# Earlier loads of keys and queries, a new schedule of the row-maxima steps and later value weights in a two-layer transformer kernel

## The chip, the cores and the metric

The kernel runs on one core of one Trainium2 chip. The metric is device time in microseconds (us) from launch to end; lower is better. The profile shows one execution, engine by engine: PE (TensorE matmuls), PEld (TensorE weight loads), DVE (VectorE), ACT (ScalarE), POOL (GpSimd), and SP, whose queue issues nearly all DMAs here.

## What is computed

The reference runs two equal layers over `x` of shape 1 x 2048 x 640 in float32. A layer is an attention block with 32 heads of 20 and an MLP:

```python
def _A_ref(x, wqkv, wo):
    qkv = (x @ wqkv).reshape(B, S, 3, H, Dh)   # transposed to 3, B, H, S, Dh
    q, k, v = qkv[0], qkv[1], qkv[2]
    scores = einsum("bhqd,bhkd->bhqk", q, k) * Dh ** -0.5
    p = softmax(scores)
    return einsum("bhqk,bhkd->bhqd", p, v) ... @ wo

x = x + _A_ref(_layernorm(x), wqkv, wo)
x = x + _B_ref(_layernorm(x), w1, b1, w2, b2)      # relu(x @ w1 + b1)^2 @ w2 + b2
x = x + _A_ref(...); x = x + _B_ref(...)           # once more, with the same weights
```

## The kernel before

A layer has three stages: the projections (`qkv`), the attention proper (`attention`), and output projection with MLP. Each float32 operand of the projections is split into a high and a low part, and three products are summed. Intermediate queries, keys and values go to DRAM (`d_qk`, `d_kd`, `d_v`) and come back in the layouts that later stages need.

**Softmax maxima.** The kernel subtracts the true row maximum inside the exponential: the maximum is an added row of the query operand of the score matmul. So every score is computed twice, first with queries on the partitions to take maxima (`by_queries`, L561; reduced on DVE, L573), then with keys on the partitions for the exponentials (`score`, L657; ACT, L664). Heads are taken in 8 groups of four (g), queries in 4 blocks of 512 (qb), keys in 4 chunks of 512 (c); `t = 4 g + qb` numbers a block of the attention, and 16 key tiles `kt` make one block.

**Maxima during the projections.** A part of the maxima is computed already during the projections. A triple (g, qb, c) is a *group* of 8 steps, each of two matmuls (one for each row half of the array). With c a number it is *plain*: two matmuls, two DVE reductions (`smax_two`, L587). With "d" or "e" it is *double* and serves two key chunks (0 and 1, or 2 and 3): the matmuls of a first half-step multiply queries with key differences `kd` and ACT writes their relu (`step_two`, L595); the second half-step multiplies with the lower chunk's keys and DVE adds the relu and takes the maximum (`both_two`, L602). `DOUBLE` holds 22 double groups of the head groups 0, 1 and 2.

**What sets the order.** The instruction order is written out by program. `qkv` walks 40 units (tb, pos), a token block with one of ten 128-column pieces of queries and keys, 15 matmul products each (n = 0 to 39), and then 16 value units of 30 products. From unit 4 on a product is two half-height matmuls, the second 22 products behind the first (`halves` L358, `catch` L367). After every product `between(cost)` (cost 1, or 0.65 in value units) lowers a pace counter; when it is used up `some()` issues one maxima step and adds `PLAIN_PACE` or `DOUBLE_PACE`. `following` takes the next group off a list and calls `tiles`, which issues the loads of its keys and queries (`load_k`, `load_q`, `load_kd`: six DMAs of 80 KB each, on SP) and also those of the following group, or of the following two while not all token blocks are transposed. `end_group` gives tiles up that no later group needs. `LISTED` and `PLAIN` say after which unit groups are listed. What is stored (`d_qk`, `d_kd`, `d_v`) is put on SP 10 products after its unit ended (`later`). After the last projection `while begun` drops the double groups that were not begun.

**Queues and tiles.** SP takes its DMAs in the order in which the program recorded them and stops at the first whose semaphores are not yet there. Tiles of keys, queries, split weights and evicted projections share one pool of 42 slots of 8 KB a partition; a new tile waits for the last reader of the slot that it gets.

**The attention.** `attention` interleaves scores (`a`, `b`), value products (`V`, L669) and the maxima that are still to do (`m`, `n`; the list `todo`), by the strings in `ORDERS`. `begin(i)` issues loads: at every fourth key tile of a head group's first block the keys of head groups ahead (`load_k`), and the keys of group 3 in block 1.

Of the kernel before, what the change touches and what calls it, by code (L numbers as in the profile page):

```python
# [25 lines left out]
NQB = S // QB  # L26
# [13 lines left out]
def tile_layers(  # L40
# [26 lines left out]
    def slot(shape, dtype, label):  # L67
        return arena.tile(shape, dtype, tag="slot", name=name(label))
# [132 lines left out]
    w_v = Split("wv", HALF, KD * 4)  # L201
# [15 lines left out]
    def raw_rows(src, k):  # L217
        raw = xtile("raw")
        dma(nc.sync, raw, src[k * P : (k + 1) * P, :])
        return raw  # L220
# [121 lines left out]
    xt_, keys = {}, {}  # L342
# [162 lines left out]
    left, done, split = {}, set(), {}  # L505
# [12 lines left out]
    def load_k(g, c, keep):  # L518

        if not keep:  # L520
            k = slot([P, 2, QB], F32R, "k")
        elif (g % 4, c) in kept:
            k = kept[g % 4, c]
        else:
            k = kept[g % 4, c] = slot([P, 2, QB], F32R, "k")
            for par in range(2):
                dma(nc.sync, k[64 * par + 60 : 64 * par + 62], d_one)
        k_t[g, c] = k
        rows_of_heads(k, d_qk[1, :, :, c * QB : (c + 1) * QB], KSEG, g)

    def load_q(t):
        g, qb = divmod(t, NQB)
        q_t[t] = slot([P, 2, QB], F32R, "q")
        rows_of_heads(q_t[t], d_qk[0, :, :, qb * QB : (qb + 1) * QB], QSEG, g)
# [202 lines left out]
    def prep_job():  # L737
# [12 lines left out]

    PLAIN = [
        ([(0, 0, 0)], [(1, 0, 0)]),
        ([(0, 0, 1)], [(1, 0, 1)]),
        ([], []),
        ([], []),
    ]
    DOUBLE = [
        [],  # L760
# [9 lines left out]

    FIRST = 4
    PLAIN_PACE = 4.2
    DOUBLE_PACE = 2.1
    LISTED = {11: 1, 14: 2, 18: 3}
    UNITS = [(tb, pos) for tb in range(NQB) for pos in range(FIRST)]
    UNITS += [(tb, pos) for pos in range(FIRST, 10) for tb in range(NQB)]

    def qkv(first, x_src, rest):

        pending, groups, work = [], [], []  # L780
        double, twos, begun = [], [], []
        left.update((t, 4) for t in range(NBLK))
        done.clear()
        state = {"pace": 0, "n": 0}
        early, late, later_rows = {}, {}, []
        coming = [y for x in DOUBLE for y in x if y[2] == "d"]

        def at(when, n, f):
            when.setdefault(n, []).append(f)

        for pos in range(2 if first else FIRST, 10):
            n = UNITS.index((0, pos)) - 4 if pos >= FIRST else pos - 2
# [8 lines left out]
        for k in range(KD if first else w_v.n):  # L801
            n = len(UNITS) - 7 + k
            if first:
                at(early, n - 2, lambda k=k: raws.append(raw_rows(wqkv[:, 2 * D :], k)))
                at(late, n, lambda k=k: w_v.put(
                    raws.pop(0), k * 4, k * 4 + 2, 2, nc.scalar.copy, pool_lo
                ))
            else:
                at(early, n, lambda k=k: w_v.load(k))

        def begin(when, n):
            for f in when.pop(n, ()):
                f()

        def later(f):
            pending.append((state["n"] + 10, f))

        def settle(n):
            while pending and pending[0][0] <= n:
# [2 lines left out]
        def tiles(x):  # L822
            g, qb, c = x
            for c in [c] if c in range(4) else [c, 2 * "de".index(c)]:
                if (g, c) not in k_t:
                    if c in range(4):
                        load_k(g, c, g > 1)
                    else:
                        load_kd(g, c)
            if g * NQB + qb not in q_t:  # L830
                load_q(g * NQB + qb)

        def end_group(x):
            g, qb, c = x
            t = g * NQB + qb
            rest = groups + double + [w[0] for w in work + twos] + [w[0][0] for w in begun]
            if t == 0:
                left[t] -= 1 if c in range(4) else 2
                if left[t] == 0:
                    mrows_max(t)  # L840
                    mrows(t)
                    later_rows.append(t)
            if (t or left[t]) and all(y[:2] != (g, qb) for y in rest):
                del q_t[t]
            use = {(y[0], y[2]) for y in rest + coming}
            use |= {(h, 2 * "de".index(y)) for h, y in use if y not in range(4)}
            for y in [y for y in k_t if y[0] == g and y not in use]:
                if g < 2 or y[1] not in range(4):
                    del k_t[y]

        def following(todo, queue):

            if not queue:
                if not todo:
                    return None
                x = todo.pop(0)
                tiles(x)
                for y in todo[: 2 if len(xt_) < NQB else 1]:
                    tiles(y)
                queue.extend((x, p, sub) for p, sub in PAIRS)  # L860
            return queue.pop(0)
# [10 lines left out]
        def some():  # L872
# [4 lines left out]
            if begun and (len(begun) > 1 or not (double or twos)):  # L877
# [6 lines left out]
                if (p, sub) == PAIRS[-1]:  # L884
                    end_group(w[0])
                return DOUBLE_PACE
            if groups or work:
# [3 lines left out]
            if w:  # L891
                (g, qb, x), p, sub = w
                begun.append((w, step_two(g * NQB + qb, p, sub, x)))
            return DOUBLE_PACE

# [11 lines left out]
        for n, (tb, pos) in enumerate(UNITS):  # L907
            while tb not in xt_:
                next(rest)
            begin(early, n)  # L910

            def end(store, n=n, tb=tb, pos=pos):
                later(store)
                if pos >= FIRST and tb == NQB - 1 or n == 4 * FIRST - 1:
                    w_qk.past(pos * 10 + 9, w_qk.got)

            proj_unit(pos, tb, run, run.whole if n < FIRST else run.halves, end)
            begin(late, n)
            if 2 < n < NQB * FIRST + 3:
                b, step = divmod(n - 3, 4)  # L920
                have, new = groups, PLAIN[b][step // 2]
                if step % 2:
                    have.extend(new)
                elif new:
                    tiles(new[0])
                if step == 2 and DOUBLE[b]:
                    tiles(DOUBLE[b][0])
            if n in LISTED:
                double.extend(DOUBLE[LISTED[n]])
                coming[:] = [y for y in coming if y not in double]  # L930
            if first:
                w_qk.save_full(1)
                w_v.save_full(1)
        for tt in range(NKT):

            def end(store, tt=tt):
                later(store)
                if tt % 4 == 3:
                    del xt_[tt // 4]

            v_unit(tt, run, end)
            if first:
                w_v.save_full(1)
            if tt == 10:
                load_v(0, 0)
            if tt == 12:
                for c in range(4):
                    assert (0, c) not in k_t
                    load_k(0, c, True)
                load_q(1)  # L950
        while run.behind:
            run.catch()
        while begun:
            del double[:], twos[:]
            some()
        w_v.drop()
        w_qk.drop()
# [22 lines left out]
    def attention(first, x_src, first_rows):  # L980
# [5 lines left out]
        state = {"begun": -1, "done": 0, "acc": None, "debt": 0, "st": ps_st}  # L986
        sm_ring = Ring(4, 5, 6)
        todo = [
            (t, p, sub, c)
            for t in range(NBLK)  # L990
            for c in range(4)
            for p, sub in PAIRS
            if (t, p, sub, c) not in done
        ]
# [13 lines left out]
        def begin(i):  # L1008

            t, u = divmod(i, NKT)  # L1010
            g, qb = divmod(t, NQB)
            if u == 1:
                q_t.pop(t - 1, None)
                if t + 2 < NBLK and t + 2 not in q_t:
                    load_q(t + 2)
            if u % 4 == 1 and qb == 0:
                k_t.pop((g - 1, u // 4), None)
                for h in (0, 1, 2, 3) if g else (0, 1, 2):
                    if g + h < NG and (g + h, u // 4) not in k_t:
                        load_k(g + h, u // 4, True)  # L1020
                if g and g + 3 >= NG:
                    del kept[(g - 1) % 4, u // 4]
            if t == 1 and u % 4 == 1:
                load_k(3, u // 4, True)
            if u in (2, 10) and qb == NQB - 1 and g + 1 < NG:
                load_v(g + 1, u // 8)
            if first and t < 16 and u % 6 == 3:
                prep_job()
            if first and t < 16 and u == 8:
                for sp in (w_o, w_1, w_2):  # L1030
                    sp.save_full()
                    sp.past(sp.count, sp.got)
            if (t, u) in loads:
                loads[t, u]()
            if t == NBLK - 1 and u == 12:
                first_rows.extend(row_tile(x_src, i) for i in range(4))
            if i in split:
                split.pop(i)()
# [300 lines left out]
```

## Time and profile before

| | |
|---|---|
| time, median of 3 runs | 3780.71 us (3778.38 to 3782.02) |
| the profiled execution: time / span | 3779.25 us / 3777.3 us |
| span, first layer: projections / attention / rest | 0 to 380 / to 1490 / to 1905 us |
| span, second layer: projections / attention / rest | to 2262 / to 3362 / to 3777 us |
| PE busy in these six stretches | 338.30, 1075.71, 408.97, 328.12, 1072.84, 409.22 us |
| ACT busy in the two attentions | 1043.02, 1042.79 us |
| granted PE clock in the six stretches | 0.96, 0.98, 1.00, 0.95, 0.98, 1.00 |

Idle time of an engine that does not set the end costs nothing. A wait is put down to the instruction or DMA that ended it; "q<-d_qk" is the load of a query tile. "Granted clock" is the share of full speed that TensorE was given.

### The profile page before, as it was taken

The page shows a single profiled execution, that of the slowest core. Times are in us where ns is not written, and L with a number is a line of the kernel's source. Part 1 is how long each engine was busy: PE and PEld are TensorE (multiplying, and loading weights), DVE is VectorE, ACT ScalarE, POOL GpSimd, SP SyncE. Part 2 cuts the span into 40 slices and gives each one's busy share as a digit, 9 for nine tenths or more (in the row PEclk, how much of TensorE's full clock was granted, in tenths as well). Part 3 has the DMA queues.
Part 4 walks back from the last instruction along what each step waited for, and adds up shares of the span by engine and source line. Part 5 has one row for each costly group of instructions (what it writes and reads, how often), then busy time and mean ns, then how long its engine had stood idle before and what let it go on. Part 6 is the DMA issues. An engine that isn't in the chain of part 4 may idle for free. (4 is left out here: it accounts for less than half of the span.)

```text
span 3777.3 us, 69873 instructions
## 1 busy us (share of the span) xinstructions
PE 3633.2 (96%) x25492; PEld 2202.4 (58%) x25492; DVE 2667.9 (71%) x5208; ACT 2698.9 (71%) x5298; POOL 867.0 (23%) x993
## 2 busy tenths in 40 slices
PE   7989799999999999999989897999999999999999
PEld 5879234444444444988878792444444444359898
DVE  7869488888888882444468784888888888814443
ACT  2768699999999997122217686999999999951221
POOL 6530134321111221111254200211112122111220
PEclk9999899999999999999999898999999999999999
DMA  6654454432222135722246543222222221357221
GB/s 212 203 195 134 112 150 144 156 101 62 69 59 56 47 92 158 285 85 70 91 144 213 162 133 86 72 64 67 80 58 65 56 57 49 95 188 256 70 71 41
DMA packets 277992, 425.92 MB, mean 113 GB/s; under 512 B 70228, under 2 KB 129364, under 8 KB 277648
## 3 DMA queue, kind: packets, MB, share of 16 engines
q1 hardware_dynamic: 277104, 419.73, 35.7%
q8 instruction: 202, 3.31, 0.4%
q10 hardware_dynamic: 544, 1.71, 0.2%
q14 instruction: 142, 1.16, 0.1%
HBM read 276.62 MB, written 144.68 MB: 112 GB/s over the span
## 5 line engine op out<-in xcount | busy, mean ns | idle before, releaser
L664 ACT ACTIVATE e<-banks 128x512 f32<-128x512 f32 x4096 | 2085.8, 614 | 120.4 <-PE banks L657 80.5
L573 DVE TENSOR_REDUCE mx<-banks 128x1 f32<-128x512 f32 x2624 | 1657.7, 685 | 385.2 <-PE banks L561 348.3
L669 PE MATMUL banks<-e,vg 128*32 128x512 f32 x8192 | 1098.8, 609 | 11.9 <-ACT e L664 11.9
L657 PE MATMUL banks<-q,k 62*128 62x512 f32 x4096 | 1076.0, 446 | 2.3 <-DVE mx L602 2.0
L657 PEld LDWEIGHTS banks<-q,k 62*128 62x128 f32 x4096 | 574.4, 185 | 854.3 <-ACT e L664 772.3
L561 PE MATMUL banks<-k,q 60*128 60x512 f32 x3424 | 1000.2, 414 | 63.2 <-DMA k<-d_qk 47.2
L561 PEld LDWEIGHTS banks<-k,q 60*128 60x128 f32 x3424 | 496.7, 188 | 193.1 <-DVE mx L573 101.3
L602 DVE CUSTOM_DVE_ANT_0 rl<-banks,rl 128x512 f32<-128x512 f32 x672 | 436.7, 689 | 102.1 <-PE banks L561 64.6
L595 ACT ACTIVATE rl<-banks 128x512 f32<-128x512 f32 x672 | 366.2, 600 | 114.1 <-PE banks L561 89.5
L669 PEld LDWEIGHTS banks<-e,vg 128*32 128x32 f32 x8192 | 161.6, 108 | 337.4 <-issue 281.3
L338 PE MATMUL banks<-w,h 128*128 128x320 f32 x2304 | 349.3, 310 | 2.7 <-DVE h L259 2.5
L338 PEld LDWEIGHTS banks<-w,h 128*128 128x128 f32 x2304 | 339.3, 188 | 11.4 <-DVE h L259 6.4
L1187 ACT ACTIVATE r<-banks,b_t 128x512 f32<-128x512 f32 x96 | 66.2, 689 | 382.1 <-PE banks L338 232.6
L358 PE MATMUL banks<-xnT,wqk 64*128 64x512 f32 x1080 | 337.8, 407 | 0.0
L367 PE MATMUL banks<-xnT,wqk 64*128 64x512 f32 x1080 | 336.6, 404 | 0.1
L338 PE MATMUL banks<-xnT,w 128*128 128x512 f32 x1440 | 331.5, 391 | 0.0
L338 PEld LDWEIGHTS banks<-xnT,w 128*128 128x128 f32 x1440 | 270.7, 189 | 55.7
L561 PE MATMUL banks<-kd,q 60*128 60x512 f32 x672 | 211.0, 408 | 34.2 <-DMA q<-d_qk 15.4
L713 POOL TENSOR_TENSOR few<-few,minus_t 128x16 f32<-128x16 f32 x62 | 179.9, 2901 | 198.5 <-DMA few<-d_s 198.5
L270 POOL CAST mr<-nt 128x32 fp32r<-128x32 f32 x64 | 13.5, 211 | 915.6 <-DVE nt L628 915.6
L724 POOL TENSOR_TENSOR o<-o 128x512 f32<-128x512 f32 x62 | 79.6, 1284 | 612.1 <-DMA o<-d_r 347.9
L367 PEld LDWEIGHTS banks<-xnT,wqk 64*128 64x128 f32 x1080 | 208.1, 193 | 15.1 <-DVE turned_t L360 0.5
(88 smaller groups left out, 2923.8 us busy)
## 6 DMA issues: line engine op xcount, KB each, us to landing
q<-d_qk SPq DMA_DIRECT2D x792, 80.0 KB
d_qk<-ev SPq DMA_DIRECT2D x80, 512.0 KB
k<-d_qk SPq DMA_DIRECT2D x456, 80.0 KB
x<-d_x SPq DMA_DIRECT2D x96, 320.0 KB
d_o<-ot SPq DMA_DIRECT2D x248, 80.0 KB
ot<-d_o SPq DMA_DIRECT2D x38, 512.0 KB
d_v<-v SPq DMA_DIRECT2D x32, 512.0 KB
vg<-d_v SPq DMA_DIRECT2D x32, 512.0 KB
```

The lines of the kernel that those rows point to most:

```text
L338: nc.tensor.matmul(dst, a, b, start=(n == 0), stop=(n == last))
L358: nc.tensor.matmul(dst, a[:64], b[:64], start=start, stop=last)
L367: nc.tensor.matmul(dst, a, b, start=False, stop=last, skip_group_check=True)
L561: nc.tensor.matmul(dst, q_t[t][b : b + 60, p, sub * P : (sub + 1) * P], k_t[t // NQB, c][b : b + 60, p, :], start=True, stop=True,)
L573: nc.vector.tensor_reduce(maxima(t)[:, 2 * p + par, sub, c : c + 1], dst, axis=AX.X, op=ALU.max)
L595: nc.scalar.activation(r, dst, AF.Relu)
L602: nc.vector.tensor_tensor_reduce(out=r[par], in0=dst, in1=r[par], scale=1.0, scalar=LEAST, op0=ALU.add, op1=ALU.max, accum_out=maxima(t)[: ...
L657: nc.tensor.matmul(dst, k_t[t // NQB, kt // 4][b : b + 62, p, (kt % 4) * P : (kt % 4 + 1) * P], q_t[t][b : b + 62, p, :], start=True, stop ...
L664: nc.scalar.activation(es[p][:, par, :], dst, AF.Exp, scale=SCALE)
L669: nc.tensor.matmul(acc[32 * h : 32 * h + 32, :], v_t[t // NQB, kt // 8][:, kt % 8, 32 * h : 32 * h + 32], es[p][:, par, :], start=(kt == 0 ...
L713: nc.gpsimd.tensor_tensor(few, few, minus_t, op=ALU.pow)
L724: nc.gpsimd.tensor_mul(o[:, 0, :], o[:, 0, :], o[:, 1, :])
```

## The change

All of it is in `qkv` and `attention`. The lists and paces become a table `STEPS`, which says after which unit a group's tiles are loaded ("tiles") or the group is listed; `DOUBLE_PACE` goes from 2.1 to 1.97; `following` always loads for the next two groups; `end_group` keeps a query tile only if one of the next four groups uses it, and otherwise it is loaded again later; stores of units from 4 on are issued 16 products after their unit and those of values 12 after; the loads of the value weights (second layer) are issued from unit 36 on, two a unit; all listed double groups are finished; the keys of head group 3 and the queries of blocks 12 and 13 are loaded after value unit 13.

```diff
-    PLAIN = [
-        ([(0, 0, 0)], [(1, 0, 0)]),
-        ([(0, 0, 1)], [(1, 0, 1)]),
-        ([], []),
-        ([], []),
-    ]
...
-    DOUBLE_PACE = 2.1
-    LISTED = {11: 1, 14: 2, 18: 3}
+    DOUBLE_PACE = 1.97
+    STEPS = {
+        2: [("tiles", (0, 0, 0))],
+        4: [("plain", (0, 0, 0)), ("tiles", (1, 0, 0))],
+        5: [("plain", (1, 0, 0))],
+        7: [("tiles", (0, 0, 1))],
+        9: [("plain", (0, 0, 1)), ("tiles", (1, 0, 1))],
+        10: [("tiles", (0, 1, "d"))],
+        11: [("plain", (1, 0, 1))],
+        12: [("double", 1)],
+        15: [("double", 2)],
+        19: [("double", 3)],
+    }
...
-                at(early, n, lambda k=k: w_v.load(k))
+                at(early, len(UNITS) - 4 + k // 2, lambda k=k: w_v.load(k))
...
-        def later(f):
-            pending.append((state["n"] + 10, f))
+        def later(f, n):
+            pending.append((state["n"] + n, f))
...
-            rest = groups + double + [w[0] for w in work + twos] + [w[0][0] for w in begun]
+            rest = [w[0] for w in work[:1] + twos[:1]] + [w[0][0] for w in begun[:1]] + groups + double
...
-            if (t or left[t]) and all(y[:2] != (g, qb) for y in rest):
+            if (t or left[t]) and all(y[:2] != (g, qb) for y in rest[:4]):
                 del q_t[t]
...
-                for y in todo[: 2 if len(xt_) < NQB else 1]:
+                for y in todo[:2]:
                     tiles(y)
...
-                later(store)
+                later(store, 10 if n < FIRST else 16)
...
-            if 2 < n < NQB * FIRST + 3:
-                b, step = divmod(n - 3, 4)
-                have, new = groups, PLAIN[b][step // 2]
-                if step % 2:
-                    have.extend(new)
-                elif new:
-                    tiles(new[0])
-                if step == 2 and DOUBLE[b]:
-                    tiles(DOUBLE[b][0])
-            if n in LISTED:
-                double.extend(DOUBLE[LISTED[n]])
-                coming[:] = [y for y in coming if y not in double]
+            for what, x in STEPS.get(n, ()):
+                if what == "tiles":
+                    tiles(x)
+                elif what == "plain":
+                    groups.append(x)
+                else:
+                    double.extend(DOUBLE[x])
+                    coming[:] = [y for y in coming if y not in double]
...
-                later(store)
+                later(store, 12)
...
+            if tt == 13:
+                for c in range(4):
+                    load_k(3, c, True)
+                for qb in range(2):
+                    load_q(3 * NQB + qb)
...
-        while begun:
-            del double[:], twos[:]
+        while double or twos or begun:
             some()
...
-                for h in (0, 1, 2, 3) if g else (0, 1, 2):
+                for h in (0, 1, 2, 3) if g else (1, 2):
...
-            if t == 1 and u % 4 == 1:
-                load_k(3, u // 4, True)
```

## The prediction

> **What bounds the kernel now.** I read the page's line of engines first, then PE's waits in the stretches that the change touches, then busy time by stretch.
>
> ```profile
> PE 3633.2 (96%) x25492; PEld 2202.4 (58%) x25492; DVE 2667.9 (71%) x5208; ACT 2698.9 (71%) x5298; POOL 867.0 (23%) x993
> ```
>
> PE is busy for 96% of the span, so what can be had is in the rest. The waits of PE in 26 to 379 us (projections, first layer), 379 to 485 (start of its attention), 1928 to 2261 and 2261 to 2365 (the same in the second layer) say for what; columns: total us, times, longest.
>
> ```profile
> PE banks L561 <- DMA q<-d_qk: 12.8, 7, 3.6
> PE banks L561 <- ACT rl L595: 7.3, 2, 6.5
> ...
> PE banks L561 <- DMA d_qk<-ev: 2.0, 2, 1.3
> ```
> ```profile
> PE banks L561 <- DMA k<-d_qk: 27.5, 4, 17.1
> ```
> ```profile
> PE banks L561 <- DMA q<-d_qk: 7.9, 5, 3.3
> PE banks L561 <- ACT rl L595: 7.5, 2, 6.6
> PE banks L561 <- DMA k<-d_qk: 5.1, 2, 4.4
> PE banks L358 <- DMA wv<-d_wv: 2.8, 1, 2.8
> PE banks L561 <- DMA d_qk<-ev: 1.1, 1, 1.1
> PE banks L561 <- DMA kd<-d_kd: 0.9, 1, 0.9
> ```
> ```profile
> PE banks L561 <- DMA k<-d_qk: 14.7, 2, 14.2
> PE banks L561 <- DMA q<-d_qk: 6.1, 1, 6.1
> ```
>
> The reader is to see one kind of wait: a maxima matmul (L561) stands in PE's fixed order before its keys or queries have landed, and all behind it waits too. Without waits the projections are bound by PE, as a stretch of the value units shows (columns: length; busy PE, PEld, DVE, ACT, POOL; granted clock):
>
> ```profile
> 290.00:379.00 89.00, 88.40 (x1032) 87.80 (x1029) 81.20 (x272) 74.20 (x148) 5.03 (x12) 1.00 0.40 130
> ```
>
> The attention is bound by ACT's exponentials. The same view of L664 alone, at the start of each attention and behind it:
>
> ```profile
> 380.00:480.00 100.00, 62.84 (x123) 0.81 0.44 117
> 480.00:1480.00 1000.00, 973.43 (x1913) 1.00 0.32 94
> 2262.00:2362.00 100.00, 70.08 (x138) 0.83 0.32 90
> 2362.00:3352.00 990.00, 965.28 (x1898) 1.00 0.25 69
> ```
>
> Behind the start an exponential takes 1000/1913 = 0.523 us and 990/1898 = 0.522. So the 123 and 138 at the start are worth 64.3 and 72.0 us, and the starts lose 35.7 and 28.0.
>
> **The change, part by part.** *1. Loads two groups ahead, queries reloaded.* I read the order of the instructions in both programs: from the recording of a query load to its first matmul, before has mostly 93 to 137 matmuls, after 191 to 259 (89 for the first double group). The maxima's query and key waits of the projections go: 12.8 and 7.9 + 5.1 + 0.9, and those put down to a store in the same queue, 2.0 and 1.1. What is late next is the matmul rate itself.
>
> Price: 16 queries are loaded again, 96 more DMAs. SP issues at the rate of this row pair, 38 DMAs from 347.61 to 361.79 + 2.46:
>
> ```profile
> 347.61 0.61 SPq L76 DMA_DIRECT2D k<-d_one  x2
> ...
> 361.79 2.46 SPq L76 DMA_DIRECT2D q<-d_qk  x6
> ```
>
> So 16.6/38 = 0.44 us each, 21 us of SP a layer. SP's own waits hide them: in the second layer's projections it stands 73.9 us for POOL alone.
>
> ```profile
> SPq L76 <- POOL ev L273: 73.9, 20, 8.1
> ...
> SPq L76 <- PE banks L561: 16.7, 14, 10.1
> ```
>
> Without that cover they would cost up to 42 us in all; I take 0.
>
> *2. Slots.* The two 6.5 us waits on ACT are not ACT's: ACT stands for a slot that a store has not left, in the second layer through POOL (rows: ACT's waits 120 to 290, POOL's 2000 to 2172).
>
> ```profile
> ACT wv L161 <- DMA d_qk<-ev: 7.1, 1, 7.1
> ```
> ```profile
> POOL ev L270 <- DMA d_qk<-ev: 33.2, 4, 13.4
> ```
>
> In before a new tile takes the slot of a store recorded 14 to 58 matmuls earlier; in after, with queries given up sooner, twice at 40 and 42, else from 66 on. So 7.3 and 7.5 go. The stores come 6 products later (2 for values): at the distance of products in PE's timeline, 0.23 us, about 1.4 us, hidden by that distance. Without that cover this term stays, at 14.8 us.
>
> ```profile
> 212.51 0.39 PE L358 MATMUL banks<-xnT,wqk 64*128 64x512 f32 x1
> ...
> 212.74 0.39 PE L358 MATMUL banks<-xnT,wqk 64*128 64x512 f32 x1
> ```
>
> *3. Value weights later* (second layer). The last load waits for a matmul 59 before its first use, in before 5. That is about 7 us against the 3.3 from issue to PE's release in before: the 2.8 goes; bounds 0 and 2.8.
>
> *4. The clock.* Behind each of these stalls PE runs at half clock (columns: length, PE busy, clock):
>
> ```profile
> 203.60:207.00 3.40, 3.40 (x20) 0.50 0.68 240
> 235.40:241.20 5.80, 5.78 (x28) 0.50 0.59 229
> ...
> 1942.50:1947.80 5.30, 5.30 (x23) 0.50 0.68 179
> 2002.50:2005.90 3.40, 3.36 (x16) 0.50 1.04 358
> 2129.60:2135.60 6.00, 6.00 (x28) 0.50 0.58 173
> ...
> sum 45.40, PE 45.31; mean PE 4.53
> ```
>
> Ten such stretches, five a layer, hold 45.31 us of PE work at half rate; at full rate it takes half, so 22.7 us go with the stalls. The first row is the smallest case, behind a stall of 2.00 us:
>
> ```profile
> 202.21 0.47 PE L561 MATMUL banks<-kd,q 60*128 60x512 f32 x1 [2.00 <-DMA q<-d_qk]
> ```
>
> The Trainium skill, "TensorE: Matmul & The Clock Gate", Part 1: The HAM clock gate, has the clock halved only after an idle window of about 3.4 us. By that rule only the three stretches behind stalls of over 4 us (5.78, 5.30, 6.00) would end with them, 8.5 us in place of 22.7, and the time would be 14 us longer. The row behind the 2.00 us stall contradicts it, so I keep 22.7.
>
> *5. Pace 1.97 and the last double group.* It moves 16 pairs of matmuls a layer from the attention, where ACT hides them (I take 0; up to 3.7 us a layer if PE bound there), into the projections, where PE is the bound: 32 x 0.23 = 7.4 us more. DVE gets 16 reductions of L602 a layer there, against 0.69 + 0.08 us each about 12 us. It is 81.20/89 = 91% busy in the value units; at 2.1/1.97 the rate of steps rises by some 4% and DVE to 95%. I take PE's 7.4; the end if DVE binds is 2 x 12 = 24. For small waits that this makes I leave 3 us a layer, an eighth of the 22 to 25 us of waits that go.
>
> *6. The attention's start.* The 17.1 and 14.2 us stalls are maxima of the last double group's second chunk, whose keys block 0 loads; the next are those of head group 3. After, that group is done and group 3 is loaded at value unit 13. Its queries for the first maximum stand behind four key tiles: 38 DMAs. SP is through with the loads of unit 12 at 364.3 us and idles between value stores until the attention begins; 38 x 0.44 more is 381, landing about 1.5 us later. The first maximum comes after six scores, near 381 us, so it waits some 2 us (0 to 7, if SP issues at the slowest six of that burst). With that and 2 us of start-up, I leave 4 of each loss: 35.7 + 28.0 - 8 = 55.7.
>
> *Sum.* Projections: 22.1 (12.8 + 7.3 + 2.0) + 25.3 + 22.7 - 7.4 - 6 = 56.7. Attention: 55.7. Together 112.4, against the profiled execution's 3779.25 us (1.5 under the median shown): 3666.9, as a median about 3668.
>
> **The rivals.**
>
> *A. The loads are earlier in the program, not in time*: SP waits for POOL's stores (73.9 us above) and reaches them as late as now. Then the query and key waits of the projections stay, 14.8 + 15.0, with about half of the clock's 22.7: 3668 + 41 = 3709. For it: SP is in order. Against: the stores ahead wait for work 40 to 50 matmuls back, the lead is 191 or more.
>
> *B. DVE binds in the value units*: 24 in place of 7.4, so 3685. For it the 91%; against it that in that stretch PE is 99% busy.
>
> *C. The DMAs of a load run one after another.* If each of the 38 took the 1.5 us from issue to landing by itself, the first maximum would come 57 - 17 = 40 us late in each attention, and the loss there would be 80 in place of 63.7: 3668 + 76 = 3744. Against it stands the 0.44 us distance. The skill's "DMA: Bandwidth & Descriptors", Bandwidth, asks for transfers of 1 MiB and up; its fixed cost of about 2.0 us a DMA (Anatomy of one DMA) speaks against adding 96 of 80 KB. Paid in full, one after another, it would give an estimated 3778; the burst's rows contradict that.
>
> *D. Slower: SP stops at the reloaded queries.* A load into a slot still read by PE holds the stores behind it, ACT and POOL find no slot, and each such stop costs PE as much as the 6.5 us wait with its half clock (2.9): 9.4 us. After has 15 such loads a layer that wait for PE in the first layer's order, before 10. If eight a layer did it: 16 x 9.4 = 150, 3668 + 150 = 3818; from six a layer on (113) the gain is gone. Against: only one of the 15 waits for a matmul behind its own place (by 8), and before's 14 waits for PE sum to 16.7.
>
> **How the numbers follow.** Forecast 0.70, A 0.12, B 0.09, C 0.02, D 0.04; 0.03 for more gain than the forecast (residual waits gone too, about 3650). A measurement of this kernel can tell about 0.2%, 7.6 us. Only D is slower (0.04); 0.02 for within, between D and C; faster 0.94. The range, 3645 to 3705, takes in the forecast with its bounds (small waits, the clock's 14, the burst) and B; A, C and D are left out, 0.18.
>
> **What would show it.** In the changed profile: the waits of L561 for q, k and d_qk in both projections under 6 us in all (step 1; A if near 30); no wait of 6 us on L595 (2); none of L358 for wv (3); granted clock 0.98 or more in 200 to 290 us (4); the first exponential near 354 in place of 380 us (5); 123 exponentials within 72 us of the attention's start, with one wait of L561 for q or k of a few us (6). Wrong would be a first exponential after 370, or SP waiting for PE far beyond 17 us a layer.

## The result and the profile after

| | time, median (runs) | ratio to before, 95% interval |
|---|---|---|
| before, measured beside it | 3781.36 us (3778.38 to 3784.58) | |
| after | 3649.7 us (3647.81 to 3652.43) | 0.9652 [0.9635, 0.9669] |

The gain is 131.7 us; 112.4 were forecast. The profiled execution of after took 3648.68 us, so 130.6 less than the one of before. Its line of engines, to be held against the one at the head of the prediction:

```profile
PE 3589.5 (98%) x25492; PEld 2180.7 (60%) x25492; DVE 2648.6 (73%) x5208; ACT 2701.7 (74%) x5330; POOL 865.5 (24%) x993
```

The matmuls are the same in number (x25492), and PE's busy time is 43.7 us less. In the projections it fell by 15.6 us, where the clock rose; in the two attentions it fell by 29.9, more than half of that in the steady part, where the clock is 1.00 in both kernels and PE counts as busy nearly all the time. PE's waits in after, in 26 to 350 us (projections, first layer), 350 to 450 (start of its attention) and 1890 to 2210 (projections and start, second layer); columns: total us, times, longest.

```profile
PE banks L453 <- DVE x L254: 2.8, 2, 1.8
PE banks L367 <- DVE turned_t L360: 2.2, 2, 1.6
PE banks L561 <- ACT rl L595: 1.2, 2, 0.8
...
PE banks L561 <- DMA q<-d_qk: 0.9, 1, 0.9
```
```profile
PE banks L561 <- DMA q<-d_qk: 2.4, 2, 2.2
```
```profile
PE banks L561 <- DMA q<-d_qk: 5.6, 3, 4.8
PE banks L358 <- DMA wv<-d_wv: 2.0, 2, 1.6
```

The waits for q, k and d_qk, 12.8 + 2.0 and 7.9 + 5.1 + 1.1 + 0.9 before, are down to 0.9 inside the first layer's projections, and the 5.6 of the second layer are mostly one of 4.8 that stands behind its projections. The stalls of 17.1 and 14.2 us on keys are gone; waits of 2.2 and 4.8 for a query stand in their place.

How much each stretch gave, from the times of the first and the last exponential of each layer:

| stretch | before, us | after, us | gain | forecast |
|---|---|---|---|---|
| to the first exponential, layer 1 | 380.3 | 348.8 | 31.4 | 26.3 |
| attention, layer 1 | 1105.7 | 1064.2 | 41.5 | 31.7 |
| rest of layer 1, projections of layer 2 | 776.6 | 747.8 | 28.8 | 30.4 |
| attention, layer 2 | 1096.1 | 1067.2 | 28.8 | 24.0 |

**Projections.** Busy time from the first product to the first exponential, layer 1 and layer 2, of before and of after; columns: stretch, length, busy us of PE, PEld, DVE, ACT, POOL with their counts, granted clock, DMA share, GB/s.

```profile
35.40:380.30 344.90, 315.03 (x2821) 282.21 (x2820) 278.82 (x850) 222.58 (x430) 131.33 (x158) 0.96 0.56 182
1932.70:2262.50 329.80, 303.76 (x2780) 280.37 (x2779) 265.12 (x819) 210.55 (x405) 93.84 (x109) 0.95 0.54 172
```
```profile
33.60:348.80 315.20, 306.77 (x2853) 278.08 (x2852) 287.06 (x883) 228.80 (x445) 131.31 (x158) 0.99 0.65 212
1862.00:2160.80 298.80, 295.63 (x2813) 279.76 (x2812) 274.17 (x851) 217.46 (x421) 92.42 (x107) 0.99 0.63 198
```

Length less PE's busy time is PE's idle time: 29.9 + 26.0 before, 8.4 + 3.2 after, so 44.3 us less. Inside these stretches PE was busy at half clock for 50.6 us before (12 stretches, 43.2 to 50.0 us the first) and for 9.3 after (69.2 to 76.1 and 2049.0 to 2052.4). Half of the difference, 20.7 us, is what the clock is worth. Busy time fell by 16.4, so some 4 us of work were added: the 32 or 33 matmuls a layer more in the counts.

**Attention.** The exponentials (L664) alone: 850 us of the steady part of after's first attention, then the two starts. The busy column is ACT's.

```profile
500.00:1350.00 850.00, 831.89 (x1641) 1.00 0.31 90
```
```profile
348.80:420.00 71.20, 64.73 (x128) 0.95 0.48 136
...
2160.80:2233.00 72.20, 62.51 (x124) 0.93 0.43 122
```

In the steady part one exponential takes 850/1641 = 0.518 us, before 0.523. The starts lose 71.2 - 128 x 0.518 = 4.9 and 72.2 - 124 x 0.518 = 8.0 us, in place of 35.7 and 28.0: a gain of 51. The other 20 us of the attentions' 70 are the steady part, which the prediction had at nothing.

### The profile page after: what moved, and what is told of

Read it like the earlier page. It is cut to its first block, busy times and chain, and to the rows that moved or that the text cites. A ratio compares the mean times of both kernels' runs of the same rounds, so it can differ in the third digit from the quotient of the medians.

```text
span 3646.9 us, 70099 instructions
## 1 busy us (share of the span) xinstructions
PE 3589.5 (98%) x25492; PEld 2180.7 (60%) x25492; DVE 2648.6 (73%) x5208; ACT 2701.7 (74%) x5330; POOL 865.5 (24%) x993
## 4 chain that ended last, share of the span: by engine, by line
PE 92%; DMA 3%; DVE 2%; ACT 2%; POOL 1%; issue 0%; SPq 0%; ACTq 0%; POOLq 0%; DVEq 0%
PE banks L669 27%; PE banks L338 21%; PE banks L657 20%; PE banks L561 14%; PE banks L367 5%; PE banks L358 4%; DMA k<-d_qk 1%; ACT e L664 1%; DMA d_qk<-ev 0%; DMA q<-d_qk 0%; SPq L76 0%; PE banks L453 0%; DVE h L259 0%; DVE r L1191 0%; ACT h L258 0%
## 5 line engine op out<-in xcount | busy, mean ns | idle before, releaser
L664 ACT ACTIVATE e<-banks 128x512 f32<-128x512 f32 x4096 | 2075.6, 616 | 57.5 <-PE banks L657 23.4
L573 DVE TENSOR_REDUCE mx<-banks 128x1 f32<-128x512 f32 x2560 | 1619.6, 685 | 354.2 <-PE banks L561 313.5
L669 PE MATMUL banks<-e,vg 128*32 128x512 f32 x8192 | 1093.9, 606 | 11.6 <-ACT e L664 11.6
L561 PE MATMUL banks<-k,q 60*128 60x512 f32 x3392 | 990.5, 413 | 11.1 <-DMA q<-d_qk 9.0
L561 PEld LDWEIGHTS banks<-k,q 60*128 60x128 f32 x3392 | 499.4, 186 | 108.3 <-DVE mx L573 71.1
L602 DVE CUSTOM_DVE_ANT_0 rl<-banks,rl 128x512 f32<-128x512 f32 x704 | 456.4, 688 | 25.8 <-PE banks L561 6.7
L595 ACT ACTIVATE rl<-banks 128x512 f32<-128x512 f32 x704 | 382.0, 601 | 58.5 <-PE banks L561 43.1
L669 PEld LDWEIGHTS banks<-e,vg 128*32 128x32 f32 x8192 | 161.3, 108 | 313.2 <-issue 260.8
L367 PE MATMUL banks<-xnT,wqk 64*128 64x512 f32 x1080 | 331.4, 396 | 1.6 <-DVE turned_t L360 1.6
L358 PE MATMUL banks<-xnT,wqk 64*128 64x512 f32 x1080 | 328.7, 396 | 0.0
L338 PEld LDWEIGHTS banks<-xnT,w 128*128 128x128 f32 x1440 | 270.7, 189 | 55.7
L367 PEld LDWEIGHTS banks<-xnT,wqk 64*128 64x128 f32 x1080 | 202.6, 188 | 12.9 <-DVE turned_t L360 2.1
L561 PE MATMUL banks<-kd,q 60*128 60x512 f32 x704 | 208.4, 397 | 1.2 <-ACT rl L595 1.2
L358 PEld LDWEIGHTS banks<-xnT,wqk 64*128 64x128 f32 x1080 | 200.1, 188 | 11.6 <-issue 2.6
```

What stands on the lines that cost most here:

```text
L338: nc.tensor.matmul(dst, a, b, start=(n == 0), stop=(n == last))
L358: nc.tensor.matmul(dst, a[:64], b[:64], start=start, stop=last)
L367: nc.tensor.matmul(dst, a, b, start=False, stop=last, skip_group_check=True)
L561: nc.tensor.matmul(dst, q_t[t][b : b + 60, p, sub * P : (sub + 1) * P], k_t[t // NQB, c][b : b + 60, p, :], start=True, stop=True,)
L573: nc.vector.tensor_reduce(maxima(t)[:, 2 * p + par, sub, c : c + 1], dst, axis=AX.X, op=ALU.max)
L595: nc.scalar.activation(r, dst, AF.Relu)
```

## The experiments

Each ran beside the kernel before; its median in the first two sets (up to the stores) was 3780.7 and 3780.0, in the third (from the slower pace on) 3777.0; the one beside after was 3781.36. So a difference of two medians from different sets is uncertain by some 4 us. The theory: two separate gains, the loads with their slots (projections and clock) and the attention's start. The rivals stand in each expectation.

### One group ahead instead of two

```diff
-                for y in todo[:2]:
+                for y in todo[: 2 if len(xt_) < NQB else 1]:
```

> The changed kernel, but once all token blocks are transposed only the next group's tiles are loaded, as before the change. If the two-groups lead is what ended the waits of the maxima for queries and keys in the projections, most of these 30 us come back with some 10 us of half clock: 3675 to 3690 us against 3650, waits of L561 for q and k in the two projections together over 15 us. If the waits only went because the slots are free and the queue on SP no longer stops, the lead does not matter: at most 3655 us.

Measured: 3657.23 us, 0.9674 [0.966, 0.9688], 7.5 us above after. PE's waits in 26 to 362 us and the busy time of both projections of this run:

```profile
PE banks L561 <- DMA q<-d_qk: 6.9, 6, 2.4
```
```profile
34.30:356.00 321.70, 310.53 (x2853) 286.50 (x2852) 287.22 (x883) 229.51 (x446) 131.29 (x158) 0.98 0.64 208
1870.40:2172.60 302.20, 296.75 (x2813) 282.52 (x2812) 274.30 (x851) 218.06 (x421) 92.25 (x107) 0.99 0.61 196
```

Waits for queries come back, 6.9 us in layer 1, and PE's idle time goes from 11.6 to 11.2 + 5.4 = 16.6. The size lies between theory and rival, nearer to the rival: the second group ahead is worth only a small part of what the projections gained.

### One group ahead, and query tiles kept

The edit above, and:

```diff
-            if (t or left[t]) and all(y[:2] != (g, qb) for y in rest[:4]):
+            if (t or left[t]) and all(y[:2] != (g, qb) for y in rest):
```

> As e1_one_ahead, and a query tile is kept while any listed group uses it, as before the change. A new tile then takes slots whose store stands up to 24 matmuls behind it. If tight slots made the two 6.5 us waits on ACT, they come back, 15 us with 6 us of half clock: 15 to 25 us over e1_one_ahead. If they were ACT's own work or came with the load lead, the time is that of e1_one_ahead within 5 us.

Measured: 3665.64 us, 0.9696 [0.9681, 0.971], 8.4 above the run before. PE's waits in 26 to 362 us, then both projections:

```profile
PE banks L561 <- ACT rl L595: 5.5, 2, 5.3
PE banks L561 <- DMA q<-d_qk: 3.6, 4, 1.2
```
```profile
34.40:360.00 325.60, 310.23 (x2853) 285.09 (x2852) 287.20 (x882) 229.13 (x446) 131.16 (x158) 0.97 0.59 193
1871.10:2179.20 308.10, 300.21 (x2813) 281.53 (x2812) 274.51 (x851) 217.66 (x422) 93.42 (x109) 0.98 0.57 181
```

The long wait on the relu's slot is back (5.3 us), and with it a lower clock: the tiles given up do free slots, for 8 us where 15 to 25 were expected. Together with the second group ahead that is 16 us.

### Keys of head group 3 late again

```diff
-            if tt == 13:
-                for c in range(4):
-                    load_k(3, c, True)
-                for qb in range(2):
-                    load_q(3 * NQB + qb)
...
+            if t == 1 and u % 4 == 1:
+                load_k(3, u // 4, True)
```

> The changed kernel, but the keys of head group 3 are loaded in block 1 of the attention as before, and nothing after value unit 13. If the large stall of the attention's start went with the last double group and only the second one (8 us at key tile 16) with the early keys, it costs 8 + 8 us less the 2.2 + 4.8 us that the first maximum waits now, and some us because the maxima are crowded into fewer key tiles: 3657 to 3670 us. If the early keys carry the whole gain at the start, both stalls are back: over 3695 us.

Measured: 3724.6 us, 0.985 [0.9833, 0.9866], 75 above after. PE's waits from 350 to 470 us, and, in the steady part from 560 to 1400 us, the exponentials (first) and the maxima's matmuls (L561, PE and PEld busy):

```profile
PE banks L561 <- DMA k<-d_qk: 34.0, 4, 26.9
```
```profile
560.00:1400.00 840.00, 818.07 (x1606) 1.00 0.30 85
```
```profile
560.00:1400.00 840.00, 306.08 (x1100) 143.77 (x1100) 1.00 0.30 85
```

The stall is there in full: it has only moved from the key tiles 12 to 16 to the tiles 16 to 20, where block 1 loads these keys. Without these early keys, finishing the last double group saves nothing at the start. And the steady part is back at 840/1606 = 0.523 us, with 16 pairs of matmuls fewer than before, so not their number but what the early keys allow sets it.

### The pace alone, on the kernel before

```diff
-    DOUBLE_PACE = 2.1
+    DOUBLE_PACE = 1.97
```

> The kernel before with one number changed: DOUBLE_PACE 1.97, by which the last double group is finished in the projections and its 16 pairs of matmuls a layer leave the attention. The start of each attention loses one of its two stalls, 22.6 and 18.3 us. If the attention's steady pitch falls because PE is its bound while it holds 11 maxima pairs per 8 key tiles (2.094 us a key tile before, 2.074 after the change), about 14 us more go: 3725 to 3737 us against 3781, and the pitch is near 2.08. If ACT alone sets the pitch, and it fell for the changed loads, the pitch stays 2.094 and the time is 3742 to 3752.

Measured: 3761.85 us, 0.995 [0.9935, 0.9965]. Neither expectation held; 19 us are gained. PE's waits at the start (350 to 470 us) and both projections:

```profile
PE banks L561 <- DMA k<-d_qk: 28.2, 3, 24.7
```
```profile
33.80:364.30 330.50, 313.79 (x2853) 283.99 (x2852) 288.31 (x886) 229.22 (x446) 131.98 (x162) 0.97 0.57 189
1920.50:2241.70 321.20, 304.53 (x2813) 284.48 (x2812) 275.43 (x855) 218.09 (x422) 94.50 (x113) 0.96 0.55 176
```

At the start nothing is gained: the stall sits at the tiles 16 to 20 as in the run above. The gain lies in the projections, 14 and 9 us shorter although 32 matmuls each were added: PE's idle time there is 16.7 + 16.7 in place of 55.9, with the waits on L595 at 2.5 and 2.1 (7.3 and 7.5 before). That the pace alone removes these was in no theory.

### Fewer maxima in the attention

The maxima of the last key chunk are left out in every second block from 13 on, 80 of 640 pairs of matmuls a layer.

```diff
-            if t in PARTLY:
+            if t in PARTLY or t % 2:
...
-            if (t, p, sub, c) not in done
+            if (t, p, sub, c) not in done and not (c == 3 and t % 2)
```

> The changed kernel without the maxima of key chunk 3 in the odd blocks from 13 on (80 of the attention's 640 pairs of matmuls a layer left out; their place in the row maximum is filled with the least number). So far 8 key tiles with 11 pairs take 8 x 2.094 us, with 10.5 pairs 8 x 2.069, 0.4 us a pair. If PE is the bound there, the pitch goes on falling with the pairs, to 2.04 at least (four exponentials at 0.509 us busy each are 2.036, where ACT would take over) or to 2.00 if ACT's floor is lower: 32 to 65 us less, 3585 to 3618. If ACT sets the pitch and it fell for another reason, the pitch stays 2.07 and the time 3645 to 3652.

Measured: 3631.2 us, 0.9607 [0.9592, 0.9621]. The same two views as above, from 2250 to 3130 us (second layer):

```profile
2250.00:3130.00 880.00, 867.54 (x1721) 1.00 0.24 65
```
```profile
2250.00:3130.00 880.00, 299.73 (x999) 149.53 (x999) 1.00 0.24 65
```

The time lies between the two expectations. The pitch fell as the first one has it: 880/1721 = 0.511 us an exponential, 2.045 a key tile where 2.04 was named. In the key tiles 8 to 16 of the run with the pace alone, where PE lacks maxima to do, sixteen exponentials take 8.14 us, 0.509 each. So the steady part lies between two limits a few per cent apart, ACT's at 0.509 and another that rises with the maxima per key tile; why it is taken for PE's is said under step 5. The second layer's attention is 15.9 us shorter than in after, the first layer's only 1.7, for a longer start and a new wait, in 400 to 1420 us:

```profile
PE banks L669 <- DMA vg<-d_v: 6.0, 2, 4.5
```

### The first query ahead of three key tiles

```diff
-                for c in range(4):
+                load_k(3, 0, True)
+                load_q(3 * NQB)
+                for c in range(1, 4):
                     load_k(3, c, True)
-                for qb in range(2):
-                    load_q(3 * NQB + qb)
+                load_q(3 * NQB + 1)
```

> The changed kernel, but after value unit 13 the queries of block 12 are loaded behind the first key tile of head group 3 and not behind all four: 24 DMAs, 10.5 us at 0.44 us each, earlier. If the first maximum of each attention waits for the end of this burst on SP, its waits (2.2 and 4.8 us) go and the first four key tiles take 10 us in place of 13.6 and 16.8: 3640 to 3646 us. If these tiles are slow for the start of the exponentials itself, the time stays within 2 us of 3650.

Measured: 3642.6 us (3637.51 to 3660.03), 0.9645 [0.962, 0.967]. The first four key tiles take 9.8 and 11.2 us in place of 13.6 and 16.8, and no wait for q is left there. The spread is wide, and the profiled run is its slowest. From 400 to 1430 us it has waits that after has not; the faster runs were not profiled, so whether these waits make the spread is not shown:

```profile
PE banks L669 <- DMA vg<-d_v: 10.0, 3, 3.6
```

### Value weights early again

```diff
-                at(early, len(UNITS) - 4 + k // 2, lambda k=k: w_v.load(k))
+                at(early, n, lambda k=k: w_v.load(k))
```

> The changed kernel with the loads of the second layer's value weights one a unit from unit 33 on, as before the change. If the 2.8 us wait for them came from the slots, it makes no difference: 3647 to 3653 us. If the later loads ended it, 3 to 5 us more with their half clock: 3653 to 3656.

Measured: 3652.09 us, 0.9662 [0.9646, 0.9679], no difference to after that the runs can tell. PE's wait in the second layer's projections (1862 to 2160 us):

```profile
PE banks L358 <- DMA wv<-d_wv: 2.8, 2, 2.3
```

2.8 us early, 2.0 in after: the edit removes little of it.

### All stores 10 products after their unit

```diff
-                later(store, 10 if n < FIRST else 16)
+                later(store, 10)
...
-                later(store, 12)
+                later(store, 10)
```

> The changed kernel with all stores of queries, keys and values 10 products after their unit, as before the change. If the loads' lead of 190 and more matmuls covers what SP loses while it waits for POOL at such a store, it makes little difference: 3645 to 3655 us. If SP's waits for POOL (73.9 us in the second layer's projections before) are what the later stores cure, the waits for queries come back: over 3660.

Measured: 3649.49 us, 0.9656 [0.9641, 0.967]: the later stores cost nothing and bring nothing.

### The slower pace with the new loads

```diff
-    DOUBLE_PACE = 1.97
+    DOUBLE_PACE = 2.1
```

> The changed kernel with DOUBLE_PACE 2.1 again in place of 1.97; everything else stays, so 21 pairs of maxima matmuls are left over and stand in a row behind the last projection of each layer. Theory (the earlier loads and the sooner freed slots take the waits away, the pace only places the last double group): the projections' waits stay as few as after the change, the leftover row costs about 10 us a layer because a half-step there waits for ACT or DVE at some 0.7 us, the projections themselves get 4 to 5 us shorter: 3655 to 3672 us. Rival (the faster pace itself takes much of the waits away, as the run with the pace alone suggests with 16 us less in the first layer's projections): waits of L561 for q and of L595's slots come back at over 10 us a layer, 3680 us or more.

Measured: 3659.24 us, 0.9686 [0.9672, 0.9701], 9.5 above after and inside the theory's range. The two projections to their last product, then the two rows of leftover maxima:

```profile
35.00:345.60 310.60, 301.54 (x2808) 280.36 (x2809) 274.27 (x838) 218.88 (x424) 131.01 (x158) 0.98 0.65 212
1872.30:2161.30 289.00, 288.06 (x2768) 270.93 (x2769) 260.95 (x807) 207.37 (x400) 92.09 (x107) 1.00 0.65 203
345.60:361.00 15.40, 14.30 (x47) 7.97 (x43) 13.69 (x43) 11.02 (x22) 0.00 (x0) 0.64 0.72 234
2161.30:2177.80 16.50, 14.18 (x49) 7.91 (x45) 13.97 (x44) 10.97 (x21) 0.00 (x0) 0.63 0.69 177
```

Idle time of PE is 9.1 + 0.9 us up to the last product and 1.1 + 2.3 in the leftover rows, against 8.4 + 3.2 in after: the waits stay away without the faster pace. So the loads remove them. What the pace does with these loads is to place the last 21 pairs: the projections of after are 4 and 9 us longer (315.2 - 0.7 and 298.8 - 0.7 to their last product) and save the leftover rows of 15.4 and 16.5 us. Of these 19 us about 11 are given back at the starts, where the first four key tiles take 10.1 and 9.5 us in this run and 13.6 and 16.8 in after; that the rows give the first query time to land is an argument only. In those rows PE counts as 93% and 86% busy, and yet the mean clock is 0.64 and 0.63.

### The start alone, on the kernel before

The pace 1.97 and, in the kernel before, the loads of the keys of group 3 and the queries of blocks 12 and 13 after value unit 13; the old lead, lists, stores and slots stay.

```diff
-    DOUBLE_PACE = 2.1
+    DOUBLE_PACE = 1.97
...
+            if tt == 13:
+                for c in range(4):
+                    load_k(3, c, True)
+                for qb in range(2):
+                    load_q(3 * NQB + qb)
...
-                for h in (0, 1, 2, 3) if g else (0, 1, 2):
+                for h in (0, 1, 2, 3) if g else (1, 2):
...
-            if t == 1 and u % 4 == 1:
-                load_k(3, u // 4, True)
```

> The kernel before with only two edits: DOUBLE_PACE 1.97, so that the last double group is done before the attention, and the keys of head group 3 and the queries of blocks 12 and 13 loaded after value unit 13. No longer lead of the loads, no tiles given up sooner, no later value weights. Theory (the start's stall is the keys of group 3, and the steady pitch follows the density of maxima that early keys allow): the run with the pace alone gave 3761.85; its stalls at key tiles 16 to 20 (about 37 and 31 us where 8.3 are due, so 29 and 22) go, and the pitch falls from 2.093 to 2.07 us a key tile, 10 to 12 us a layer; the projections keep their waits for q and ACT. That is 3762 - 51 - 22 = 3689; range 3675 to 3697. Rival (the stall only moves on again, or the pitch stays at 2.093): over 3705.

Measured: 3688.81 us, 0.9763 [0.9749, 0.9778]; 3689 was expected. The exponentials from 500 to 1350 us, then both projections:

```profile
500.00:1350.00 850.00, 831.82 (x1640) 1.00 0.32 90
```
```profile
34.20:365.80 331.60, 314.87 (x2853) 281.71 (x2852) 287.72 (x883) 229.27 (x445) 131.24 (x158) 0.96 0.58 188
1879.50:2201.90 322.40, 305.46 (x2813) 284.84 (x2812) 274.53 (x851) 218.00 (x422) 92.03 (x107) 0.96 0.54 174
```

The steady part is at after's 0.518 us, the start's stall is gone, and the projections are those of the run with the pace alone (33.7 us idle). So, the last double group being finished, the early keys alone carry the attention's gain, start and steady part. The table, loads, stores and slots are worth the remaining 3688.8 - 3649.7 = 39 us (42 by the ratios to before), all in the projections.

### Value tiles eight key tiles earlier

In this form on after (the second run), and together with the first query ahead of three key tiles (the first run):

```diff
-            if u in (2, 10) and qb == NQB - 1 and g + 1 < NG:
-                load_v(g + 1, u // 8)
+            if (qb, u) in ((NQB - 2, 10), (NQB - 1, 2)) and g + 1 < NG:
+                load_v(g + 1, qb - NQB + 2)
```

> The changed kernel with the query of block 12 ahead of the last three key tiles of head group 3, and with the value tiles of the next head group loaded 8 key tiles sooner (at key tiles 10 of the third block and 2 of the fourth, in place of 2 and 10 of the fourth). Theory (in the first layer's attention SP's queue is the second limit: the value tiles came down to 4 to 13 us ahead of their use with the change and to nothing with the query first, which gave waits of L669 for vg): no wait of L669 for vg, the gain at the start stays, 3634 to 3643 us with a narrow spread. Rival (the value tiles are late because SP stops for POOL, wherever they stand): waits of L669 for vg stay at several us and the time at 3643 to 3652.

> The changed kernel with only the value tiles of the next head group loaded 8 key tiles sooner. Theory (with the change they are still 4 us or more ahead of their use, so nothing waits for them): no difference that can be told, 3645 to 3652 us. Rival (they already cost something that the waits do not show): under 3643.

Measured: with the query first 3641.71 us (3640.86 to 3642.98), 0.964 [0.9626, 0.9655]; on after alone 3653.55 us (3651.09 to 3655.53), 0.9669 [0.9653, 0.9685]. The exponentials in the 16 us from 350 to 366, of after and of the first of the two:

```profile
350.00:366.00 16.00, 10.49 (x21) 0.79 0.70 226
```
```profile
350.00:366.00 16.00, 15.55 (x31) 1.00 0.69 230
```

31 exponentials in place of 21, at full clock: the start runs without a loss. No wait of L669 for vg is left in either run, and the spread is 2 us in place of 22. That is the fastest full kernel here, 8 us under after by the medians. Some 4 of these are the kernel before, which was faster in this set, and the intervals of the two ratios overlap, so its size against after is not settled. Against the second run, which stands in the same set and differs by the query alone, it is 11.8 us faster, and no run of the one reaches the other. The earlier value tiles alone gain nothing; their time lies 1.6 us above the expected range.

## Why the prediction was right, and where it was not

**The sum.** 112.4 us forecast, 131.7 measured, inside the range. The projections gave 60.2 where 56.7 were forecast, the attention 70.3 where 55.7 were. That 3649.7 still lies within a range that begins at 3645 is luck in part: some 20 us of the gain were in no term of the sum, and the 0.03 for a time near 3650 stood for another reason.

**Steps 1 to 4 together: right in size.** Idle time 44.3 (forecast 22.1 + 25.3 - 6 = 41.4), clock 20.7 (22.7), added work about 4 (7.4). The waits of L561 and L595 in the changed profile's projections are as said there.

**How they divide: wrong.** PE's idle time in both projections, from the rows above, as parts of the change are added one after another (the time with the start's keys early is from the third set of runs):

| kernel | PE idle, us | time, us |
|---|---|---|
| before | 55.9 | 3780.7 |
| pace 1.97 | 33.4 | 3761.9 |
| and the start's keys early | 33.7 | 3688.8 |
| and the table of steps, later stores and value weights | 23.3 | 3665.6 |
| and query tiles given up | 16.6 | 3657.2 |
| and two groups ahead (after) | 11.6 | 3649.7 |

The second group ahead brings 7.5 us, the slots 8.4, the table with its earlier first loads and later issues 23 to 25. The later stores and the later value weights, taken back alone, made no difference to after; so most of the 23 probably belongs to the table, but it was not run alone. The parts are not independent: the pace removes 22.5 us of idle time with the old loads, and with the new ones it removes none (10.0 to the last product with the old pace). Both take the same waits. Why the faster pace does so by itself was not tested; that another slot now meets another store is an argument only.

**Step 3** failed: 2.0 of the 2.8 us stay, and with the loads early again they are 2.8, so moving them is worth 0.8 at most.

**Step 4** held. The prediction's 8.5 us by the other rule left out the stall of 3.6 us, with which it is 10; 20.7 were measured. The rule of the Trainium skill, "TensorE: Matmul & The Clock Gate", Part 1: The HAM clock gate, that the clock is halved after an idle window of some 3.4 us, is contradicted again, if idle means 3.4 us without work: in after, a wait of 2.24 us for a query ends at 352.69 us, 2.6 us of idle time with the one ahead of it, and the clock is at half for the next 6 us; in the second layer 0.38 and 1.58 us of waits for wv, by 2049.45 us, are followed by half clock until 2052.4 (busy time by stretch, PE first):

```profile
349.00:352.60 3.60, 0.98 (x2) 0.37 (x2) 0.00 (x0) 2.87 (x6) 0.00 (x0) 0.99 0.60 165
352.60:354.60 2.00, 1.75 (x4) 0.78 (x4) 0.69 (x1) 1.08 (x2) 0.00 (x0) 0.50 0.62 198
354.60:356.60 2.00, 2.00 (x10) 0.20 (x9) 1.03 (x3) 0.01 (x1) 0.46 (x2) 0.50 0.98 366
356.60:358.60 2.00, 2.00 (x11) 1.15 (x8) 0.75 (x2) 1.17 (x3) 0.00 (x0) 0.50 1.01 406
...
2050.00:2052.00 2.00, 2.00 (x14) 1.95 (x12) 1.34 (x4) 0.00 (x0) 1.09 (x2) 0.50 0.93 335
```

In these traces a stretch at half clock lasts some 3.4 us or a multiple of it (203.6 to 207.0 in before, 352.6 to 359.4 and 2049.0 to 2052.4 in after), and the 3.4 us ahead of these three held 1.40, 0.98 and 1.89 us of busy PE. Not every short stall does it: in before a wait of 1.35 us ends at 128.97, the 3.4 us to 128.6 held 2.42 us of busy PE, and the clock stays at 1.00.

**Step 5** was the one that failed by size: "16 pairs of matmuls a layer from the attention, where ACT hides them (I take 0; up to 3.7 us a layer if PE bound there)". The steady part gained 0.0055 us in each of some 1920 exponentials, 10.6 us a layer. Two things were wrong in it. The attention is not bound by ACT alone: without maxima an exponential takes 0.509 us, and the 0.523 of before hold 0.014 us more. The sign stood in the prediction's own row, ACT busy for 973.43 of 1000 us. The waits of ACT and of DVE, whose work grows with the maxima too, in before from 483 to 1400 us:

```profile
ACT e L664 <- PE banks L657: 6.0, 25, 0.3
ACT e L664 <- PE banks L561: 1.1, 2, 0.8
```
```profile
DVE mx L573 <- PE banks L561: 120.4, 337, 1.1
DVE mx L573 <- PE banks L657: 8.0, 36, 0.4
```

Both wait for PE, and for PE no wait is listed there; so the second limit is read as PE's. Its busy share alone cannot tell: it is 916.91 of 917 us in this stretch, and also 16.00 of 16.00 from 383 to 399 us in the run with the pace alone, where no maxima are done. And it is not the 16 pairs that count, but when the maxima can begin. The rows of L561 and L664 in before and after, 500 to 1400 and 500 to 1350 us:

```profile
500.00:1400.00 900.00, 876.51 (x1719) 1.00 0.31 91
```
```profile
500.00:1400.00 900.00, 335.56 (x1184) 157.48 (x1184) 1.00 0.31 91
```
```profile
500.00:1350.00 850.00, 314.62 (x1086) 151.12 (x1086) 1.00 0.31 90
```

A key tile has four exponentials, and a pair is two L561 matmuls. So before has 1184/1719 x 2 = 1.38 pairs a key tile, after 1086/1641 x 2 = 1.32, the run with late keys 1100/1606 x 2 = 1.37 and the run with fewer maxima 999/1721 x 2 = 1.16; the exponential takes 0.524, 0.518, 0.523 and 0.511 us in this order of kernels. With the keys of group 3 at hand from the first key tile, the same maxima are spread over more key tiles.

**Step 6** was right in what it removes, 51 of 55.7, and in the time of the first maximum's wait (2.2 and 4.8 us, bounds 0 to 7), but left the half clock behind that wait out of the sum. The finished last double group ("that group is done") is not enough: alone it moved the stall by four key tiles (the runs with the pace alone and with late keys). The early keys without it were not run.

**The rivals.** A and C would have left waits for q of about 30 us or a first maximum 40 us late; 0.9 us inside the first layer's projections, 2.2 and 4.8 us at the starts. D: its sign, SP waiting for PE far beyond 17 us a layer, is not there; SP waits for L561 7.4 and 7.5 us in after's projections. B lies between: against the run with the slower pace the projections are 13 us longer for 42 pairs, 0.31 us a pair with its waits, where 0.23 was taken and DVE's bound was 0.75; against before some 4 us of work came with 32 pairs.

## What to carry to other kernels

When a stall ends on a load, ask which load the next work needs: finishing the stalled work ahead of time only moved the stall to the next late load here, and moving that load removed it. Where two engines are within a few per cent of each other, taking work from the one that is "not the bound" can still gain: see whether the bounding engine is idle for a few per cent in the steady stretch and who ends its waits, and count the work per unit. When loads and a pace each remove waits, price them together; the second one finds them gone.

## What was not expected of the chip and its queues

- One exponential of 128 x 512 comes every 0.509 us where PE has no maxima to do, and 0.511, 0.518 and 0.523 us at 1.16, 1.32 and 1.37 pairs of maxima a key tile.
- A row of maxima alone, with PE 93% busy by the profile, runs at a mean clock of 0.64: 1.00 up to 349.8 us, then 0.50.
- A faster attention used up SP's cover in the first layer: at the first three changes of the head group there were 20 to 30 us from the issue of a value tile's load to its first use before, 6 to 16 after, and 4 to 11 with the query first, some of them with a wait; in the second layer 26 us and more in all three.
